# Attention and a top-1 mixture of experts on one core: the last batch's slots enter the slot product as one-hot matmuls, and the table of the other batches is read during attention

## The chip, the cores and the metric

One Trainium2 chip, one of its cores. The metric is the device time in microseconds (us) of one execution; lower is better. The core has TensorE (PE in the profile, with its weight loads as PEld), VectorE (DVE), ScalarE (ACT), GpSimd (POOL) and the sync engine SP, which issues most of the transfers.

## The reference

Four batches of eight heads attend over 768 positions with a cluster mask; the result, 3,072 tokens of 512 numbers, goes through a mixture of 16 experts in 4 groups, one expert per token.

```python
mask = q_assign[:, :, :, None] == k_assign[:, :, None, :]
scores = np.where(mask, scale * q @ k.T, -1e9)
attn = softmax(scores);  x = (attn @ v) as [3072, 512]
g_idx = argmax(x @ w_group);  g_w = softmax(x @ w_group)[g_idx]
e_idx = argmax(x @ w_expert[g_idx]);  e_w = softmax(...)[e_idx]
out = g_w * e_w * (relu(x @ w1[g, e]) @ w2[g, e])
```

## The kernel before

**Attention and routing.** The batches are attended one after the other. After each batch its 768 tokens (6 blocks of 128, one token per partition) are routed in `Router.decide`: the group and expert logits give a one-hot row of 16 experts per token (`roe`, 128 x 6 x 16), a matmul with triangular ones gives each token's rank within its expert (`psm<-roe,low`, and `psm<-roe,ones`), VectorE adds the expert's base (`rps`), and the row number in a table is the sum (`rds`, as integers `rdi`). Six indirect transfers on GpSimd's queue (`table<-pay,rdi`, L685) write token number and gate (`pay`) into that row. The table lies in device memory, one stretch of rows per expert.

**The first expert.** After batch 2 of 0 to 3 is routed, `Experts.first` chooses the expert f0 with the most tokens so far, loads its weights in four chunks for each of w1 and w2 while batch 3 is attended, reads its rows of the table (`tabA`, then integers `idA`), gathers its tokens and transposes them (`xTA`). Once batch 3 is attended, `part_a` runs f0's layers on these tokens (288 columns): 8 groups of 12 matmuls `psh<-xTA` (L963), each closed by a ScalarE eviction `hh` (L965, the upper half of the split number) and a VectorE eviction `hl` (L966, the lower half, which needs `hh`); then 4 groups of 24 matmuls `psy` (L985) over 288 columns. `psh` has three PSUM banks: a fourth group needs a bank that an earlier group's `hl` has read.

**What runs beside it.** Batch 3 is routed at the same time (`decide(B - 1, early=X.order)`); its tokens of f0 become one-hot rows in `slots_b` (`st`, 6 of 128x128 on VectorE, L1107; `o16` on ScalarE) and are collected by matmuls in `tokens_b`. `order` ranks the other 15 experts by their load (`gt`, `rank`, `pr`, `pe`, `ef`, `ei`, `perm`); `ei` is read by SP, whose loads of the later experts' weights (`st<-w`, L767) need it.

**The slot product.** `slots_b` ends with the read of the first 384 rows of every expert from the table (`tb`, L1113). The read waits for all scatters, those of batch 3 too. `slots`, called at step 13 of the 16 (0 to 15) of `part_a`'s loop, multiplies `tb` by the permutation `perm` (`psm<-perm,tb`, L1143: 6 matmuls in f32, 12 in the trace), which gives for every rank and row a token number and a gate as columns (`ri`, `rg`), and these drive the gathers `xg<-xbuf,ri` (L925) of the next expert.

**Order.** The program is written in one sequence, and a scheduler fixes each engine's order when the kernel is built: it moves instructions of `part_a` ahead of `decide` and `slots_b` where their buffers allow it. A tile name is a ring of buffers (`hh` has two), handed out in the order of the code. At run time each engine's instructions start in the built order, except that weight loads may run ahead.

Of the kernel before, what the change touches and what calls it, by code (L numbers as in the profile page):

```python
# [11 lines left out]
F16 = mybir.dt.float16  # L12
BF16 = mybir.dt.bfloat16
F32 = mybir.dt.float32
I32 = mybir.dt.int32
AF = mybir.ActivationFunctionType
ALU = mybir.AluOpType
AX = mybir.AxisListType
# [4 lines left out]
P = 128  # L23
# [6 lines left out]
PSM = "psm"  # L30
FIRST = 2
LAND = 4

def attention(ctx, tc, qT, kT, vr, cen, R, DEN, cfg):
    nc = tc.nc
# [493 lines left out]
class Router:  # L529
# [98 lines left out]
    def decide(self, b, early=None, then=None):  # L628
        nc, sm, E = self.nc, self.sm, self.E
        T = self.N // self.B // P  # L630
        t0 = b * T
# [7 lines left out]
        nc.vector.tensor_reduce(out=mw, in_=eq, axis=AX.X, op=ALU.max)  # L639
        nc.vector.tensor_tensor(out=oh, in0=eq, in1=mw.broadcast_to([P, G, 4]), op=ALU.is_equal)  # L640
        oh = oh.rearrange("p (t g) x -> p t g x", g=5)
        oe = sm.tile([P, T, 4, 4], F16, name="roe")
        og = sm.tile([P, T, 4], F32, name="rog")
        nc.vector.tensor_copy(out=og, in_=oh[:, :, 0])
        nc.vector.tensor_tensor(out=oe, in0=oh[:, :, 1:5], in1=og.broadcast_to([P, T, 4, 4]), op=ALU.mult)
# [34 lines left out]
        for c in range(T):  # L680
# [3 lines left out]
            with self.tc.issue_after(self.cfg["lo"].ins) if self.apart and not early and "lo" in self.cfg else ExitStack():  # L684
                d = self.last["p"] = nc.gpsimd.indirect_dma_start(  # L685
                    out=self.table, out_offset=bass.IndirectOffsetOnAxis(ap=di[:, c:c + 1], axis=0),
                    in_=self.pay[:, t0 + c], in_offset=None)
# [21 lines left out]
class Experts:  # L709
# [95 lines left out]
    def first(self):  # L805

        nc, R, E = self.nc, self.R, self.R.E
        t = self.small("ft", [P, E])
        m = self.small("fm", [P, 1])
        nc.vector.tensor_tensor(out=self.cntA, in0=R.cb, in1=R.ebase, op=ALU.subtract)  # L810
        nc.vector.scalar_tensor_tensor(out=t, in0=self.cntA, scalar=float(2 * E), in1=self.io, op0=ALU.mult, op1=ALU.subtract)
        nc.vector.tensor_reduce(out=m, in_=t, axis=AX.X, op=ALU.max)
        nc.vector.tensor_scalar(out=self.oh0, in0=t, scalar1=m, scalar2=None, op0=ALU.is_equal)
        nc.vector.tensor_tensor(out=t, in0=self.oh0, in1=self.io, op=ALU.mult)
        nc.vector.tensor_reduce(out=self.f0f, in_=t, axis=AX.X, op=ALU.add)
        nc.vector.tensor_copy(out=self.f0i, in_=self.f0f)

        nc.vector.tensor_scalar(out=t, in0=R.cb, scalar1=-1.0, scalar2=float(E * R.BS), op0=ALU.mult, op1=ALU.add)
        nc.vector.tensor_tensor(out=t, in0=t, in1=self.oh0, op=ALU.mult)
        nc.vector.tensor_tensor(out=R.cb, in0=R.cb, in1=t, op=ALU.add)  # L820
        yield
        self.f0 = self.load_reg(self.f0i[0:1, 0:1], E - 1)
        self.WA = self.wtiles(self.wa, 0)
        chunks = []
        for q in range(4 + LAND):
            if q < 4:
                chunks.append(self.load_chunk(0, self.f0, q))
            if q >= LAND:
                yield from self.split_beside(chunks[q - LAND], *self.WA, 0, q - LAND)
            for _ in range(FIRST):  # L830
                yield

        CA, KD = self.CA, R.KD
        nt = -(-CA // P)
        sz = [min(P, CA - t * P) for t in range(nt)]
        tab = self.small("tabA", [P, nt, 2])
        tv = R.table.rearrange("(e s) w -> e s w", s=R.BS)[bass.ds(self.f0, 1)].rearrange("e s w -> (e s) w")
        w2A = [self.load_chunk(1, self.f0, q) for q in range(4)]
        self.WA += self.wtiles(self.wa, 1)
        while R.done < R.B - 2:  # L840
            yield
        for t, n in enumerate(sz):
            R.reads(nc.sync.dma_start(out=tab[0:n, t], in_=tv[t * P:t * P + n]))
        for _ in range(FIRST + 8):
            yield
        ids = self.small("idA", [P, nt], I32)
        g = self.small("gA", [P, nt])
        for t, n in enumerate(sz):
            nc.vector.tensor_copy(out=ids[0:n, t:t + 1], in_=tab[0:n, t, 0:1])
            nc.vector.tensor_scalar(out=g[0:n, t:t + 1], in0=tab[0:n, t, 1:2], scalar1=1.0 / (XS * WS * WS), scalar2=None, op0=ALU.mult)  # L850
        self.colsA = [g[0:n, t:t + 1] for t, n in enumerate(sz)], [ids[0:n, t:t + 1] for t, n in enumerate(sz)]

# [207 lines left out]
    def order(self):  # L1060

        nc, R, E = self.nc, self.R, self.R.E
        sm = self.small
# [6 lines left out]
        nc.vector.scalar_tensor_tensor(out=key, in0=self.oh0, scalar=-1e7, in1=key, op0=ALU.mult, op1=ALU.add)  # L1070
        gt = sm("gt", [P, E, E], F16)
        nc.vector.tensor_tensor(out=gt, in0=key.unsqueeze(1).broadcast_to([P, E, E]), in1=key.broadcast_to([P, E, E]), op=ALU.is_gt)
        rank = sm("rank", [P, E])
        nc.vector.tensor_reduce(out=rank, in_=gt, axis=AX.X, op=ALU.add)
        pr = self.pr = sm("pr", [1, E, E])
        iob = self.io[0:1].broadcast_to([1, E, E])
# [12 lines left out]
        perm = sm("perm", [E, E])  # L1089
# [4 lines left out]
    def slots_b(self):  # L1094
        nc, R, E = self.nc, self.R, self.R.E

        T = R.rows.shape[1]
# [10 lines left out]
        nc.scalar.copy(out=self.o16, in_=o32)  # L1108
        self.o32, self.pb = o32, pb
        next(self.fill)  # L1110
        nt = self.nt = -(-max(self.caps) // P)
        self.tb = self.stage2.tile([P, 2, 512], F32, name="tb", bufs=1).rearrange("p a b -> p (a b)")[0:E, 0:2 * nt * P].rearrange("e (s w) -> e s w", w=2)
        R.reads(nc.sync.dma_start(out=self.tb, in_=R.table.rearrange("(e s) w -> e s w", s=R.BS)[0:E, 0:nt * P]))  # L1113

    def tokens_b(self):

# [19 lines left out]
    def slots(self):  # L1136

        nc, R, E, perm, tb, nt = self.nc, self.R, self.R.E, self.perm, self.tb, self.nt
        tps = self.R.psm.tile([P, 512], F32, name="psm")
        tpv = tps[:, 0:2 * nt * E].rearrange("p (w t e) -> p w t e", w=2, t=nt)  # L1140
        for t_ in range(nt):
            for w in range(2):
                nc.tensor.matmul(out=tpv[:, w, t_], lhsT=tb[:, t_ * P:(t_ + 1) * P, w], rhs=perm, start=True, stop=True)  # L1143
        self.ids, self.gates = self.columns([tpv[:, 0], tpv[:, 1]], [P, nt, E], "r")
        self.xg0 = self.gathers(0)

# [229 lines left out]
def tile_cluster_attention_moe(ctx, tc, qT, kT, vr, cen, wr, w1, w2, out):  # L1376
# [32 lines left out]
    ga = X.part_a()  # L1409
    for _ in R.decide(B - 1, early=X.order):  # L1410
        pass
    X.slots_b()
    for i, _ in enumerate(ga):
        with tc.issue_after(X.mm.ins):
# [42 lines left out]
```

## Time and profile before

| | us |
|---|---|
| median of 3 runs | 775.78 (771.64 to 777.94) |
| span of the profiled execution | 768.7 |
| time of the profiled execution | 770.8 |
| PE busy in it | 724.7 (94%) |
| DVE busy | 598.9 (78%) |
| POOL busy | 495.7 (64%) |
| ACT busy | 444.6 (58%) |
| 416.8 to 443.9: PE busy | 26.76 of 27.10 |
| 443.9 to 449.15: PE busy | 0.00 of 5.25 |

Attention ends at about 416.8 us; `part_a` and the routing of batch 3 fill 416.8 to 457.3 us, and the other fifteen experts the rest. Each row of a timeline gives the start, the time from first start to last end of a run of like instructions, engine, line, operation, what it writes and reads, and in brackets the idle time before it with what ended that. On VectorE and TensorE instructions overlap in the pipeline, so the step from one start to the next is what each costs in a queue without gaps.

### The profile page before, as it was taken

To read this page: it belongs to the slowest core of one execution; us is meant where nothing else is said; L and a number is where in the kernel's file an instruction comes from. 1 tells how busy PE (TensorE), PEld (TensorE's weight loads), DVE (VectorE), ACT (ScalarE), POOL (GpSimd) and SP (SyncE) were. 2 spreads that over 40 slices of the span, in tenths; PEclk is the share of its full clock that TensorE was granted. 3 is DMA by queue.
4 is the path that set the end of the run, shared out by engine and by line. 5 is a ranking of instruction groups with operands and counts; after the bars stand their busy time and mean duration, and the time that the engine had idled before them with its cause. 6 is when DMAs were issued, how large, how long until landed. Compare 5 with 4: busy or idle time off the path is not lost. (4 is left out here: it accounts for less than half of the span.)

```text
span 768.7 us, 26315 instructions
## 1 busy us (share of the span) xinstructions
PE 724.7 (94%) x10882; PEld 619.0 (81%) x10882; DVE 598.9 (78%) x1194; ACT 444.6 (58%) x877; POOL 495.7 (64%) x522
## 2 busy tenths in 40 slices
PE   5898999999999999997898979999999999999996
PEld 3676888888888888876776857888779999999896
DVE  5997988899798988996665545868588988888761
ACT  4567867677686777755674246444534455555542
POOL 9568687889978998787852435426555555554433
PEclk9999999999999999999989979999999999999998
DMA  8759647467653765407422487866677788788721
GB/s 248 190 157 217 161 125 158 111 145 185 125 162 91 173 146 104 97 12 178 127 63 61 55 269 275 275 210 216 226 245 239 255 255 274 256 279 276 248 75 49
DMA packets 115719, 134.75 MB, mean 175 GB/s; under 512 B 34963, under 2 KB 85651, under 8 KB 115592
## 3 DMA queue, kind: packets, MB, share of 16 engines
q1 hardware_dynamic: 109820, 119.61, 56.7%
q0 software_dynamic: 5616, 13.35, 4.9%
q8 instruction: 87, 1.43, 0.8%
q14 instruction: 40, 0.33, 0.2%
q10 hardware_dynamic: 156, 0.03, 0.0%
HBM read 93.20 MB, written 14.11 MB: 140 GB/s over the span
## 5 line engine op out<-in xcount | busy, mean ns | idle before, releaser
L354 POOL TENSOR_TENSOR pl<-p 128x512 f16<-128x512 f32 x278 | 285.6, 1047 | 80.8 <-ACT p L352 75.8
L308 DVE TENSOR_REDUCE mpart<-psc 128x1 f32<-128x512 f32 (+1 forms) x282 | 190.0, 683 | 29.2 <-PE psc L305 28.5
L352 ACT ACTIVATE p<-psf 128x512 f32<-128x512 f32 x288 | 168.5, 593 | 76.5 <-PE psf L348 69.4
L373 PE MATMUL pso<-V,p 128*128 128x65 f16 x1152 | 164.0, 195 | 0.0
L373 PE MATMUL pso<-V,pl 128*128 128x65 f16 x1152 | 163.2, 195 | 0.0
L374 PE MATMUL pso<-V,p 128*128 128x64 f16 x1152 | 162.9, 192 | 0.0
L374 PE MATMUL pso<-V,pl 128*128 128x64 f16 x1152 | 162.6, 192 | 0.0
L347 PE MATMUL psf<-A 82*128 82x384 f16 (+2 forms) x576 | 145.9, 278 | 6.4 <-ACT p L352 3.8
L348 PE MATMUL psf<-B 128*128 128x384 f16 (+2 forms) x576 | 146.1, 278 | 0.0
L374 PEld LDWEIGHTS <-p 128*128 128x128 bf16 x1152 | 113.6, 99 | 21.1 <-issue 1.0
L373 PEld LDWEIGHTS <-p 128*128 128x128 bf16 x1152 | 113.2, 98 | 12.6 <-issue 4.6
L305 PE MATMUL psc<-A 80*128 80x512 f16 (+1 forms) x376 | 109.9, 334 | 5.3 <-DVE mpart L308 4.2
L374 PEld LDWEIGHTS <-pl 128*128 128x128 f16 x1152 | 113.7, 99 | 0.6 <-issue 0.2
L373 PEld LDWEIGHTS <-pl 128*128 128x128 f16 x1152 | 112.1, 97 | 0.3
L966 DVE SCALAR_TENSOR_TENSOR hl<-psh,hh 128x160 f16<-128x160 f32 (+14 forms) x136 | 50.2, 371 | 60.5 <-ACT hh L965 60.1
L965 ACT ACTIVATE hh<-psh 128x160 f16<-128x160 f32 (+14 forms) x136 | 46.5, 347 | 62.5 <-PE psh L963 62.2
L963 PE MATMUL psh<-xT,wh0a 128*128 128x288 f16 (+7 forms) x512 | 74.7, 255 | 0.0
L348 PEld LDWEIGHTS <-B 128*128 128x128 f16 x576 | 57.4, 100 | 15.8 <-issue 6.6
L925 POOL DMA_INDIRECT xg<-xbuf,ri x32 | 42.2, 1318 | 40.9 <-issue 19.8
L963 PE MATMUL psh<-xT,wh0b 128*128 128x272 f16 (+6 forms) x448 | 65.2, 254 | 1.3 <-DVE xT L937 0.7
L347 PEld LDWEIGHTS <-A 82*128 82x128 f16 x576 | 56.2, 99 | 11.5 <-DMA A<-mr 2.2
L963 PE MATMUL psh<-xT,wl0a 128*128 128x288 f16 (+7 forms) x256 | 64.0, 255 | 0.0
(303 smaller groups left out, 1688.4 us busy)
## 6 DMA issues: line engine op xcount, KB each, us to landing
st<-w SPq DMA_DIRECT2D x128, 512.0 KB
B<-parts SPq DMA_DIRECT2D x64, 192.0 KB
kx<-kT SPq DMA_DIRECT2D x16, 384.0 KB
qx<-qT SPq DMA_DIRECT2D x16, 384.0 KB
vx<-vr SPq DMA_DIRECT2D x16, 384.0 KB
A<-parts SPq DMA_DIRECT2D x32, 192.0 KB
xbuf<-xs SPq DMA_DIRECT2D x16, 384.0 KB
A<-mk SPq DMA_DIRECT2D x56, 24.0 KB
```

The lines of the kernel that those rows point to most:

```text
L305: last["mm"] = nc.tensor.matmul(out=pc[:, off:off + k1 - k0], lhsT=QA[h % 8][0:80, c * P:(c + 1) * P], rhs=KA[h % 8][0:80, k0:k1], start=T ...
L308: nc.vector.tensor_reduce(out=(mp[:, 0, 0:1], mp[:, :, 1], mp[:, 1, 0:1])[i], in_=pc.rearrange("p (a x) -> p a x", a=n), axis=AX.X, op=ALU ...
L347: nc.tensor.matmul(out=o, lhsT=KA[h % 8][0:82, ks], rhs=QA[h % 8][0:82, q0:q1], start=True, stop=False)
L348: nc.tensor.matmul(out=o, lhsT=KBs[h][:, ks], rhs=QBs[h][:, q0:q1], start=False, stop=True)
L352: cfg["exp"] = nc.scalar.activation(out=p32, in_=pf, func=AF.Exp, scale=QK / (SQ * SQ))
L354: lo = (nc.vector if u in (EARLY if h < 2 else DVE_LO[h % 8] if h < NH - 2 else DVE_END) else nc.gpsimd).tensor_tensor(out=pl, in0=p32, in ...
L373: nc.tensor.matmul(out=O[:, col:col + 65], lhsT=p[:, bs], rhs=vh, start=c == 0 and q == 0 and i == 0, stop=False, skip_group_check=True)
L374: nc.tensor.matmul(out=O[:, col:col + 64], lhsT=p[:, bs], rhs=vl, start=False, stop=c == NCH - 1 and i == 1, skip_group_check=True)
L925: self.got = nc.gpsimd.indirect_dma_start(out=xg[0:n].rearrange("p k a x -> p (k a x)"), out_offset=None, in_offset=bass.IndirectOffsetOnA ...
L963: self.mm = nc.tensor.matmul(out=ph[:, 0:M], lhsT=w[:, k, fs], rhs=xT[:, a, k], start=i == 0, stop=i == 3 * KD - 1)
L965: nc.scalar.activation(out=hh[:, f], in_=ph[:, 0:M], func=AF.Relu)
L966: self.ev = nc.vector.scalar_tensor_tensor(out=hl[:, f], in0=ph[:, 0:M], scalar=0.0, in1=hh[:, f], op0=ALU.max, op1=ALU.subtract)
```

## The change

- `tb` is no longer read after the last scatters. It is read in `first`, during the attention of batch 3, right behind `tabA`; it waits only for the scatters of the batches before, and holds no row of batch 3. Both reads come `SENT` = 4 steps of the attention loop later than before, and the steps behind them are 4 fewer.
- `slots_new`, called between `decide` and `slots_b`, makes the missing rows from what VectorE holds: `oS`, one row of 288 per token that is 1 at the token's row within its expert (6 comparisons 128x288 with a 128-wide scalar per block, in a buffer of the `hh` ring), and `sw`, one row of 16 ranks per token times token number and gate, each in three parts that bf16 holds (128x576).
- `slots` adds 54 small matmuls (3 row tiles x 6 blocks x 3 parts, 32 columns each) into the same PSUM tile as the six of `perm` and `tb`.
- The loads of f0's w2 chunks are written one after each split of a w1 chunk, no longer all four behind the last.

```diff
+SENT = 4
@@ first
-        chunks = []
+        chunks, w2A = [], []
...
+            if q >= LAND:
+                w2A.append(self.load_chunk(1, self.f0, q - LAND))
...
-        w2A = [self.load_chunk(1, self.f0, q) for q in range(4)]
         self.WA += self.wtiles(self.wa, 1)
         while R.done < R.B - 2:
             yield
+        for _ in range(SENT):
+            yield
         for t, n in enumerate(sz):
             R.reads(nc.sync.dma_start(out=tab[0:n, t], in_=tv[t * P:t * P + n]))
-        for _ in range(FIRST + 8):
+        nt = self.nt = -(-max(self.caps) // P)
+        self.tb = self.small("tb", [R.E, nt * P, 2])
+        R.reads(nc.sync.dma_start(out=self.tb, in_=R.table.rearrange("(e s) w -> e s w", s=R.BS)[0:R.E, 0:nt * P]))
+        for _ in range(FIRST + 4):
             yield
@@ slots_b: the allocation and read of tb are taken out
+    def slots_new(self):
...
+        io = self.small("io16", [P, S], F16)
+        nc.gpsimd.iota(io, [[1, S]], base=0, channel_multiplier=0, allow_small_or_imprecise_dtypes=True)
...
+        x = self.small("sx", [P, T, E])
+        nc.vector.tensor_tensor(out=x, in0=oe, in1=R.ebase.unsqueeze(1).broadcast_to([P, T, E]), op=ALU.mult)
+        s = self.small("sslot", [P, T])
+        nc.vector.tensor_reduce(out=s, in_=x, axis=AX.X, op=ALU.add)
+        nc.vector.tensor_tensor(out=s, in0=R.rows, in1=s, op=ALU.subtract)
+        self.oS = self.xp.tile([P, T, S], F16, name="hh")
+        for c in range(T):
+            nc.vector.tensor_scalar(out=self.oS[:, c], in0=io, scalar1=s[:, c:c + 1], scalar2=None, op0=ALU.is_equal)
...
+        nc.vector.tensor_tensor(out=x, in0=oe, in1=self.rank.unsqueeze(1).broadcast_to([P, T, E]), op=ALU.mult)
+        rho = self.small("srank", [P, T])
+        nc.vector.tensor_reduce(out=rho, in_=x, axis=AX.X, op=ALU.add)
+        nc.vector.tensor_tensor(out=x, in0=self.io.unsqueeze(1).broadcast_to([P, T, E]), in1=rho.broadcast_to([P, T, E]), op=ALU.is_equal)
+        self.sw = self.small("sw", [P, T, 6, E], BF16)
+        nc.vector.tensor_tensor(out=self.sw, in0=x.unsqueeze(2).broadcast_to([P, T, 6, E]), in1=vals.rearrange("p t i w -> p t (i w)").broadcast_to([P, T, 6, E]), op=ALU.mult)
@@ slots
-                nc.tensor.matmul(out=tpv[:, w, t_], lhsT=tb[:, t_ * P:(t_ + 1) * P, w], rhs=perm, start=True, stop=True)
+                nc.tensor.matmul(out=tpv[:, w, t_], lhsT=tb[:, t_ * P:(t_ + 1) * P, w], rhs=perm, start=t_ + w == 0, stop=False, skip_group_check=True)
+        for t_ in range(nt):
+            for c in range(T):
+                for i in range(3):
+                    lhsT = self.oS[:, c, t_ * P:min((t_ + 1) * P, self.oS.shape[2])]
+                    nc.tensor.matmul(out=tpv[0:lhsT.shape[1], :, t_], lhsT=lhsT, rhs=self.sw[:, c, 2 * i:2 * i + 2], start=False, stop=c == T - 1 and i == 2, skip_group_check=True)
@@ main
+    X.slots_new()
     X.slots_b()
```

The built order of the two kernels differs at three places, shown as rows of that order; lines of the changed kernel stand a little lower in the file (L973 there is L966 here, L970 is L963, L1114 is L1107).

VectorE, from the end of the routing of batch 3, in the kernel before (`hl` is the eviction of `part_a`, `yl` that of its second layer; `xN` counts equal rows in a row):

```order
L1107 TENSOR_SCALAR st<-sl,rds 128x128
L1077 TENSOR_TENSOR pr<-rank,io 1x256
L1086 TENSOR_TENSOR dg<-rank,identf 16x16
L966 SCALAR_TENSOR_TENSOR hl<-psh,hh 128x288
L1079 TENSOR_TENSOR pe<-pr,io 1x256
L1088 TENSOR_REDUCE rc<-dg 16x1
L966 SCALAR_TENSOR_TENSOR hl<-psh,hh 128x288
L1081 TENSOR_REDUCE ef<-pe 1x16
L1090 TENSOR_SCALAR perm<-io,rc 16x16
L1083 CAST ei<-ef 1x16
L966 SCALAR_TENSOR_TENSOR hl<-psh,hh 128x288 x2
L989 SCALAR_TENSOR_TENSOR yl<-psy,yh 128x288 x2
```

The same place in the changed kernel:

```order
L1090 CAST ei<-ef 1x16
L1139 TENSOR_SCALAR hh<-io_11141,sslot 128x288
L1142 TENSOR_TENSOR sg<-pay,svals 128x6
L1146 TENSOR_TENSOR sx<-roe,rank 128x96
...
L1148 TENSOR_REDUCE srank<-sx 128x6
...
L1149 TENSOR_TENSOR sx<-io,srank 128x96
L1114 TENSOR_SCALAR st<-sl,rds 128x128
L1151 TENSOR_TENSOR sw<-sx,svals 128x576
L1114 TENSOR_SCALAR st<-sl,rds 128x128 x4
L973 SCALAR_TENSOR_TENSOR hl<-psh,hh 128x288 x8
L996 SCALAR_TENSOR_TENSOR yl<-psy,yh 128x288 x2
```

Before, four of the eight `hl` stand ahead of `rps` and the other four between the rows of `order`; now all eight stand in one run behind the last row of the routing, of `slots_new` and of `slots_b`.

TensorE, around the rank matmuls of batch 3, before (with what each row waits for):

```order
L963 MATMUL psh<-xTA,wl_9285 128x288
L662 LDWEIGHTS low
L662 MATMUL psm<-roe,low 128x96 [waits DVE_49]
L664 LDWEIGHTS ones
L664 MATMUL psm<-roe,ones 128x80
...
L666 MATMUL psm<-roe,ones 128x16
L963 LDWEIGHTS wh_9284
L963 MATMUL psh<-xTA,wh_9284 128x288
```

And in the changed kernel:

```order
L970 MATMUL psh<-xTA,wl_9285 128x288
L663 LDWEIGHTS low
L663 MATMUL psm<-roe,low 128x96 [waits DVE_49]
...
L667 MATMUL psm<-roe,ones 128x16
L992 LDWEIGHTS wh_10114 [waits DMASW3_49,DMASW2_49,DMASW4_49,DVE_49,PE_49]
L992 MATMUL psy<-hh,wh_10114 128x288 [waits Activation_49]
...
L970 LDWEIGHTS wh_9284
L970 MATMUL psh<-xTA,wh_9284 128x288 [waits DVE_49]
```

Before, 54 `psh` matmuls (four and a half groups) stand ahead of the rank matmuls and more follow at once; now 36 (three groups) stand ahead, six `psy` follow, and the 37th `psh` waits for VectorE.

SP, from the end of the table reads of attention on, in the changed kernel:

```order
L847 DMA tabA<-table 128x2
L335 DMA A_171<-mr 1x6x128
L847 ISA
L847 DMA tabA<-table 32x2
L850 DMA tb<-table 16x768
L335 DMA A_172<-mr 1x6x128
L875 DMA_TRANSPOSE xTA<-qx 128x8x128
...
L804 TENSOR_LOAD ei
L804 ISA x2
L768 ISA
L768 DMA st<-w 128x2x512
```

Before, `tb<-table` stood behind the fifth `st<-w` of the stream; now it stands here, behind one row `A<-mr` and the third `tabA`. The rows of f0's w2 loads ahead of this place (L767 before, L768 now, 128x4x256) stand in the same order in both kernels. Fourteen of the loads of `ei`, which stood between later weight loads, now stand between the fifth and the sixth.

## Rows read from the trace of the kernel before

**Rows 1.** The waits of TensorE from 416 to 470 us: who waited, on what, us in total, how often, longest.

```profile
PE psm L1143 <- DMA tb<-table: 5.3, 1, 5.3
```

**Rows 2.** The chain of waits that ended last, from 434 to 458 us: start, us, what.

```profile
434.80 11.10 DMA table<-pay,rdi
...
446.01 3.01 DMA tb<-table
...
449.15 2.71 PE psm L1143 x12
451.86 5.45 PE psy L985 x24
```

**Rows 3.** Busy time of each engine in stretches around that wait: the stretch and its length, then busy us and instructions of PE, PEld, DVE, ACT and POOL, the granted TensorE clock as a share of 2.4 GHz, the share of the DMA engines and GB/s.

```profile
416.80:443.90 27.10, 26.76 (x273) 21.24 (x269) 14.38 (x57) 9.19 (x18) 8.40 (x10) 1.00 0.42 80
443.90:449.15 5.25, 0.00 (x0) 0.03 (x1) 1.88 (x4) 2.79 (x4) 0.00 (x0) 0.74 0.87 226
...
452.00:455.00 3.00, 3.00 (x14) 1.93 (x13) 2.85 (x5) 0.00 (x0) 1.71 (x2) 0.50 0.56 164
455.00:458.00 3.00, 3.00 (x28) 2.26 (x27) 0.23 (x1) 0.67 (x2) 2.39 (x3) 0.72 0.86 299
```

**Rows 4.** TensorE's timeline just ahead of that wait.

```profile
440.94 1.45 PE L1129 MATMUL psm<-pb,st 128*128 128x2 f32 x12
442.25 0.65 PE L985 MATMUL psy<-hh,wl 128*128 128x288 f16 x4
442.74 1.14 PE L985 MATMUL psy<-hl,wh 128*128 128x288 f16 x8
```

**Rows 5.** TensorE's timeline around the rank matmuls of batch 3, 425 to 430 us.

```profile
425.07 0.20 PE L662 MATMUL psm<-roe,low 128*128 128x96 f16 x1
...
425.41 0.41 PE L963 MATMUL psh<-xTA,wh 128*128 128x288 f16 x2
...
429.08 1.02 PE L985 MATMUL psy<-hh,wh 128*128 128x288 f16 x7
```

**Rows 6.** VectorE's timeline from 423 to 432 us, rows of the routing of batch 3 and of part_a.

```profile
423.86 0.46 DVE L966 SCALAR_TENSOR_TENSOR hl<-psh,hh 128x288 f16<-128x288 f32 x1 [0.19 <-ACT hh L965]
...
424.76 0.26 DVE L645 TENSOR_TENSOR roe<-psm,rog 128x96 f16<-128x96 f32 x1
...
425.59 0.26 DVE L669 TENSOR_TENSOR rps<-psm,cb 128x96 f32<-128x96 f32 x1
...
428.07 0.42 DVE L1072 TENSOR_TENSOR gt<-key 128x256 f16<-128x256 f32 x1
428.41 0.18 DVE L1103 COPY pb<-pay 128x6 f32<-128x6 f32 x1
428.50 0.27 DVE L1107 TENSOR_SCALAR st<-sl,rds 128x128 f32<-128x128 f32 x1
...
429.03 0.42 DVE L1107 TENSOR_SCALAR st<-sl,rds 128x128 f32<-128x128 f32 x1
429.22 0.41 DVE L1077 TENSOR_TENSOR pr<-rank,io 1x256 f32<-1x256 f32 x1
...
429.64 0.44 DVE L966 SCALAR_TENSOR_TENSOR hl<-psh,hh 128x288 f16<-128x288 f32 x1
430.01 0.40 DVE L1079 TENSOR_TENSOR pe<-pr,io 1x256 f32<-1x256 f32 x1
...
431.24 0.16 DVE L1083 CAST ei<-ef 1x16 int32<-1x16 f32 x1
```

**Rows 7.** VectorE's timeline at 417 us, one row whose input and output are f16 and the row behind it.

```profile
417.20 0.20 DVE L883 TENSOR_SCALAR back<-ident 128x128 f16<-128x128 f16 x1
417.31 0.17 DVE L1102 TENSOR_SCALAR pb<-pay 128x6 f32<-128x6 f32 x1
```

**Rows 8.** The same view of stretches as rows 3, for three us soon after another wait of TensorE, and that wait and the restart in TensorE's timeline.

```profile
409.00:412.00 3.00, 3.00 (x26) 2.13 (x25) 1.18 (x2) 2.04 (x5) 1.85 (x2) 0.50 0.00 0
...
407.50 0.41 PE L963 MATMUL psh<-xTA,wh 128*128 128x288 f16 x2 [2.38 <-DMA xTA<-vx]
```

**Rows 9.** TensorE's timeline in attention, a run of the router's small matmuls and the row behind it.

```profile
412.97 0.60 PE L609 MATMUL psm<-WR,xTr 128*128 128x20 f16 x18
413.43 0.22 PE L347 MATMUL psf<-A 82*128 82x128 f16 x1
```

**Rows 10.** The first use of the slot product on VectorE, the first and the third gather that follow on GpSimd, and the matmuls that transpose the gathered rows on TensorE (timelines of the three engines).

```profile
451.90 0.21 DVE L1053 CAST ri<-psm 128x48 int32<-128x48 f32 x1 [6.12 <-PE psm L1143]
...
452.99 1.60 POOL L925 DMA_INDIRECT xg<-xbuf,ri  x1 [15.09 <-issue]
...
456.15 0.88 POOL L925 DMA_INDIRECT xg<-xbuf,ri  x1 [0.30 <-issue]
...
462.21 1.35 PE L935 MATMUL psm<-ident,xg 128*128 128x128 f16 x24
```

**Rows 11.** Busy time in later stretches, columns as in rows 3.

```profile
470.00:600.00 130.00, 129.94 (x1162) 106.73 (x1160) 98.61 (x145) 57.33 (x109) 64.35 (x54) 1.00 0.73 235
...
615.00:690.00 75.00, 74.94 (x924) 74.34 (x922) 64.53 (x100) 39.84 (x85) 43.96 (x41) 1.00 0.84 265
690.00:735.00 45.00, 43.09 (x597) 42.28 (x594) 37.59 (x59) 22.95 (x54) 21.42 (x22) 1.00 0.81 266
```

**Rows 12.** VectorE's timeline during the attention of batch 3, at the first use of tabA.

```profile
382.77 0.15 DVE L849 CAST idA<-tabA 128x1 int32<-128x1 f32 x1 [4.10 <-DMA tabA<-table]
```

More of the change, by code (lines that the diff above doesn't have):

```diff
@@ L641, in decide @@
         oh = oh.rearrange("p (t g) x -> p t g x", g=5)
-        oe = sm.tile([P, T, 4, 4], F16, name="roe")
+        oe = self.oe = sm.tile([P, T, 4, 4], F16, name="roe")
         og = sm.tile([P, T, 4], F32, name="rog")
@@ L1072, in order @@
         nc.vector.tensor_tensor(out=gt, in0=key.unsqueeze(1).broadcast_to([P, E, E]), in1=key.broadcast_to([P, E, E]), op=ALU.is_gt)
-        rank = sm("rank", [P, E])
+        rank = self.rank = sm("rank", [P, E])
         nc.vector.tensor_reduce(out=rank, in_=gt, axis=AX.X, op=ALU.add)
@@ L1110, in slots_b @@
         next(self.fill)
-        nt = self.nt = -(-max(self.caps) // P)
-        self.tb = self.stage2.tile([P, 2, 512], F32, name="tb", bufs=1).rearrange("p a b -> p (a b)")[0:E, 0:2 * nt * P].rearrange("e (s w) -> e s w", w=2)
-        R.reads(nc.sync.dma_start(out=self.tb, in_=R.table.rearrange("(e s) w -> e s w", s=R.BS)[0:E, 0:nt * P]))
+    def slots_new(self):
+        nc, R, E = self.nc, self.R, self.R.E
+        T = R.rows.shape[1]
+        t0 = R.N // P - T
+        S = max(self.caps)
+        oe = R.oe.rearrange("p t g x -> p t (g x)")
+        io = self.small("io16", [P, S], F16)
+        nc.gpsimd.iota(io, [[1, S]], base=0, channel_multiplier=0, allow_small_or_imprecise_dtypes=True)
+        vals = self.small("svals", [P, T, 3, 2], BF16)
+        nc.gpsimd.memset(vals, 0.0)
+        nc.gpsimd.iota(vals[:, :, 0, 0], [[P, T]], base=-P * T, channel_multiplier=0, allow_small_or_imprecise_dtypes=True)
+        nc.gpsimd.iota(vals[:, :, 1, 0], [[0, T]], base=0, channel_multiplier=1, allow_small_or_imprecise_dtypes=True)
+        x = self.small("sx", [P, T, E])
[6 more added lines that the diff above has]
+            nc.vector.tensor_scalar(out=self.oS[:, c], in0=io, scalar1=s[:, c:c + 1], scalar2=None, op0=ALU.is_equal)
+        g = self.small("sg", [P, T])
+        nc.vector.tensor_copy(out=vals[:, :, 0, 1], in_=R.pay[:, t0:t0 + T, 1])
+        nc.vector.tensor_tensor(out=g, in0=R.pay[:, t0:t0 + T, 1], in1=vals[:, :, 0, 1], op=ALU.subtract)
+        nc.vector.tensor_copy(out=vals[:, :, 1, 1], in_=g)
+        nc.vector.tensor_tensor(out=g, in0=g, in1=vals[:, :, 1, 1], op=ALU.subtract)
+        nc.vector.tensor_copy(out=vals[:, :, 2, 1], in_=g)
+        nc.vector.tensor_tensor(out=x, in0=oe, in1=self.rank.unsqueeze(1).broadcast_to([P, T, E]), op=ALU.mult)
[4 more added lines that the diff above has]
+        nc.vector.tensor_tensor(out=self.sw, in0=x.unsqueeze(2).broadcast_to([P, T, 6, E]), in1=vals.rearrange("p t i w -> p t (i w)").broadcast_to([P, T, 6, E]), op=ALU.mult)
@@ L1142, in slots @@
             for w in range(2):
-                nc.tensor.matmul(out=tpv[:, w, t_], lhsT=tb[:, t_ * P:(t_ + 1) * P, w], rhs=perm, start=True, stop=True)
+                nc.tensor.matmul(out=tpv[:, w, t_], lhsT=tb[:, t_ * P:(t_ + 1) * P, w], rhs=perm, start=t_ + w == 0, stop=False, skip_group_check=True)
+        T = R.rows.shape[1]
+        for t_ in range(nt):
[3 more added lines that the diff above has]
+                    nc.tensor.matmul(out=tpv[0:lhsT.shape[1], :, t_], lhsT=lhsT, rhs=self.sw[:, c, 2 * i:2 * i + 2], start=False, stop=c == T - 1 and i == 2, skip_group_check=True)
         self.ids, self.gates = self.columns([tpv[:, 0], tpv[:, 1]], [P, nt, E], "r")
```

## The prediction

> **What bounds the kernel now.** I read the waits of TensorE first, then the chain that ended last, then the windows, then the timelines of the engines that meet there. Of all that TensorE waits for between 416 and 470 us one wait counts, 5.3 us of the slot product for `tb` [rows 1]. The chain says what is behind it: the last scatter takes 11.10 us to land, the read of `tb` starts at 446.01 only then, and the twelve f32 matmuls and 24 `psy` that follow take 2.71 and 5.45 us [rows 2]. Ahead of the wait TensorE is busy for 26.76 of 27.10 us at full clock, in it not at all; after it the granted clock is 0.50 (1.2 GHz) from 452 to 455 us and 0.72 to 458 [rows 3]. At full clock such work is cheaper: twelve f32 matmuls take 442.25 - 440.94 = 1.31 us, four `psy` 442.74 - 442.25 = 0.49, which is 0.1225 us each [rows 4]. So the wait costs 5.27 us by the end of `psy` before and the start behind (5.3 in the view), and the low clock (2.71 - 1.31) + (5.45 - 24 x 0.1225) = 1.4 + 2.5 = 3.9 us. From 470 to 600 and from 615 to 690 us TensorE is busy to within 0.1 us each, from 690 to 735 to within 1.9 [rows 11]: what is won or lost at 417 to 460 us arrives at the end almost whole, and at most some 2 us of a loss can be swallowed there.
>
> **What the change removes.** `tb` now waits for scatters of earlier batches alone and is read next to `tabA`, whose first use is at 382.77 [rows 12], 66 us ahead of the slot product at 449.15 [rows 2]. The 5.27 us go, and with them the cause of that low clock: -5.3 and -3.9.
>
> **What it moves.** The built order shows a price on the other side. `oS` takes a buffer of the `hh` ring ahead of `part_a`, and all eight `hl` now stand behind the routing, `slots_new` and `slots_b` on VectorE. Before, four stood ahead of `rps` and four in between. TensorE has three `psh` banks; its 37th `psh` needs the first `hl`. I work out when that comes.
>
> When VectorE gets there. `roe` started at 424.76, behind an `hl` at 423.86 that had 0.19 us of idle ahead of it and steps by 430.01 - 429.64 = 0.37 [rows 6]. Without these 0.56 us it starts at 424.20, and `rps`, 0.83 us behind it before, at 425.03. From `rps` (425.59) to the start of `ei` (431.24) are 5.65 us [rows 6]; two `hl` of 0.37 stand in it, and `ei` itself adds 0.08 (the estimate for a tiny row; `pb` of 128x6 steps by 0.09), so the old chain without `hl` is 5.0 us. It contains the six `st`.
>
> What `slots_new` adds to it. Six rows of 128x6 at 0.09 us are 0.5. Four of 128x96, between 0.09 and the 0.34 of `gt` 128x256 (428.41 - 428.07), I take at 0.2: 0.8. `sw`, 128x576, goes by the slope between `st` 128x128 (429.22 - 429.03 = 0.19) and `gt`: 0.34 + 320/128 x 0.15 = 0.7 [rows 6]. The six one-hots of 128x288 are dear or cheap: by that slope 0.19 + 160/128 x 0.15 = 0.38 each as f32 rows, and not below the 0.11 of the f16 `back` 128x128 (417.31 - 417.20) [rows 7]. They read and write f16, so I take 0.2, nearer to that row: 1.2 us, with ends 0.7 and 2.3. Sum 5.0 + 0.5 + 0.8 + 0.7 + 1.2 = 8.2 us, from 7.7 to 9.3. The first `hl` starts at 425.03 + 8.2 = 433.2 and takes 0.44 [rows 6]: the 37th `psh` runs at about 433.7, between 433.2 and 434.8.
>
> A rule weighed. The one-hots at 0.11 to 0.38 are the only durations here with a page against them. The Trainium skill, "VectorE: DVE Perf Modes", says in its mode table that a `tensor_scalar` in 16 bits within SBUF handles four elements a cycle, and in its errata section that such an instruction takes 58 cycles and the elements over that factor, at 0.96 GHz: an estimate of 0.135 us each, 0.8 in all instead of 1.2, and the sum below would be +6.0 instead of +6.4. The same page gives f32 rows a factor of two, an estimate of 0.13 us for `st`, where the trace has 0.19 [rows 6]; so the trace does not bear it out throughout.
>
> What TensorE does until then. Before, the row behind the rank matmuls came at 425.41, with 54 `psh` done [rows 5]. Now 36 are done, so 18 x 0.1225 = 2.2 us of that work is not there, and six `psy` (0.74 us; seven go in 1.02 with the last one's drain [rows 5]) are. Without any wait the work ahead of the 37th `psh` would end at 425.41 - 2.2 + 0.74 = 423.95. TensorE therefore idles 433.7 - 423.95 = 9.8 us, from 9.2 to 10.9, of which about 1.6 us lie ahead of the rank matmuls (425.07 - 2.2 = 422.87, and `roe` has to be there) and the rest behind them. ScalarE's `hh` of the first three groups wait no longer than that. The `psh` and `psy` that were to hide the routing are the same matmuls as before; they only come later.
>
> The clock after it. The restart follows an idle time longer than the 5.27 us that cost 3.9. The lower bound is a wait of 2.38 us at 407.50, after which the clock was 0.50 for all of 409 to 412: 1.5 us lost at the least [rows 8]. The nearest row is the long wait, so I take 3.9.
>
> What it adds on TensorE. 54 matmuls of 32 columns. Eighteen of 20 columns took 413.43 - 412.97 = 0.46 us, 26 ns each [rows 9]: 1.4 us, and twice that, 2.8, as the upper end. Nothing hides them.
>
> The gathers. They start once `ri` is there: `ri` at 451.90, third gather issued at 456.15, its rows used at 462.21 without an idle time ahead [rows 10]. Those 10.3 us held the 24 `psy` at half clock; at full clock they hold 2.5 us less. How much of that was slack the trace does not say: 0 to 2.5, and I take 0.5 because the transposes did not wait.
>
> What costs nothing. The scatters still run on GpSimd, and nobody waits for `table` at that point now. The fourteen `ei` loads stand between the fifth and the sixth weight load, where SP stood waiting for the scatters until 446.01 [rows 2]; the cover is that wait, and the sixth load is no later than before as long as they take under some 10 us. The w2 loads of f0 stand in the same order on SP: 0. The read of `tb` in attention stands behind reads for which VectorE waits 4.10 us anyway [rows 12].
>
> **Sum.** -5.3 - 3.9 + 9.8 + 3.9 + 1.4 + 0.5 = +6.4 us. With all lower ends: -9.2 + 9.2 + 1.5 + 1.4 = +2.9; with all upper ends: -9.2 + 10.9 + 3.9 + 2.8 + 2.5 = +10.9. The profiled execution took 770.8 us, so it becomes 777.2. It lies 5.0 us under the median of the runs (775.78), so the median becomes 782.2, I say 782.
>
> **Rivals.**
> Faster: the first `hl` is no bound, and only the removed wait is left, with the 54 matmuls: -5.3 - 3.9 + 1.4 = -7.8, 768.0 for the median. For it speaks that the wait for `tb` is certain to go. Against it, the order on VectorE is fixed and TensorE has only three banks. The point that decides is when the first `hl` ends: with equal clocks the account is even at 5.3 - 1.4 - 0.5 = 3.4 us of new idle time, so at 427.3 us; `rps` at 425.03 leaves 2.3 us for a chain of which 5.0 are old rows.
> Slower still: the one-hots go at the f32 price and the third gather is late, which TensorE then waits for a second time: 6.4 + 1.1 + 2.0 = +9.5, 785.3. For it speaks that the transposes had no idle time before; it decides when VectorE's chain exceeds 9 us and the gathered rows land later than 24 full-clock `psy` allow.
> No difference: the later reads in attention are there when VectorE asks. The 4.10 us of VectorE [rows 12] shrink and with them the wait of 2.38 us and at least 1.5 us of low clock [rows 8], at most -4.10 - 2.38 - 1.5 = -8.0 against +6.4: -1.6, 774.2. Against it: the conversion of `tabA` stands as close behind the read as before.
>
> **How the numbers follow.** Forecast 0.58, with 778.7 to 786.7 as its own range; slower still 0.17; faster 0.13; no difference 0.12. One per cent, 7.8 us, is about what a measurement of this kernel can tell from no change. The forecast's +6.4 lies inside it, and about 0.17 of its 0.58 above. So: faster 0.13 and a little of the rest, 0.15; slower 0.17 + 0.17 = 0.34; same 0.51. The range reaches from 770, which takes in "no difference" and leaves out most of "faster", to 788, above the upper ends by about one.
>
> **What the changed profile would show.** TensorE's waits from 416 to 470 us: none on `tb`; instead `psh` waiting for `hl`, 7.5 to 9.5 us in one piece that ends at 433 to 435 us. VectorE's timeline: eight `hl` in a row behind `st`, no idle time of note from `rps` to them, one-hots stepping by about 0.2. Windows: clock 0.50 for several us after the restart, and not after 447. The 54 matmuls in about 1.4 us. Wrong I would be if the first `hl` came before 428 us, or if the clock stayed at 1.00 after the idle time, which alone would be worth 3.9 us.

## The result and the profile after

The changed kernel takes 779.68 us (median of 20 runs, 774.37 to 783.15), the kernel before 772.62 us on the same chip (20 runs, 766.40 to 779.58): a ratio of 1.008 over the runs, 95% interval 1.0059 to 1.0101, so about 6.2 us slower (the two medians differ by 7.1). The prediction said +6.4 us. In every ratio here, runs more than 1.5% above the fastest of the same kernel are left out as disturbed. The profiled execution of the changed kernel has a span of 776.4 us against 768.7, a time of 778.2 against 770.8.

The waits of TensorE from 405 to 475 us in the changed kernel, the largest four (who waited, on what, us in total, times, longest); they answer to [rows 1]:

```profile
PE psh L970 <- DVE hl L973: 8.3, 4, 6.8
PE psh L970 <- DMA xTA<-vx: 2.4, 1, 2.4
PE psm L663 <- DVE roe L646: 1.0, 1, 1.0
PE psy L992 <- ACT hh L972: 0.9, 1, 0.9
```

The wait on `tb` is gone. In its place stands one of 6.8 us on the first `hl`, with 1.0 us ahead of the rank matmuls and 0.9 us ahead of the six `psy`; the wait for `xTA` is the old one [rows 8].

VectorE's timeline of the changed kernel, the rows that answer to [rows 6]:

```profile
424.22 0.26 DVE L646 TENSOR_TENSOR roe<-psm,rog 128x96 f16<-128x96 f32 x1
...
425.12 0.26 DVE L670 TENSOR_TENSOR rps<-psm,cb 128x96 f32<-128x96 f32 x1 [0.16 <-PE psm L667]
...
427.47 0.30 DVE L1139 TENSOR_SCALAR hh<-io,sslot 128x288 f16<-128x288 f16 x1
427.68 0.42 DVE L1079 TENSOR_TENSOR gt<-key 128x256 f16<-128x256 f32 x1
...
432.22 0.76 DVE L1151 TENSOR_TENSOR sw<-sx,svals 128x576 bf16<-128x576 f32 x1
432.90 0.94 DVE L1114 TENSOR_SCALAR st<-sl,rds 128x128 f32<-128x128 f32 x4
433.68 1.18 DVE L973 SCALAR_TENSOR_TENSOR hl<-psh,hh 128x288 f16<-128x288 f32 x3
```

`roe` starts at 424.22, `rps` at 425.12, and from there VectorE works without a gap until the first `hl` at 433.68, 8.56 us later. A one-hot steps by 0.21 us here (427.68 - 427.47), `sw` by 0.68.

TensorE's timeline of the changed kernel at the same place and at the slot product; it answers to [rows 4] and [rows 5]:

```profile
425.92 1.42 PE L992 MATMUL psy<-hh,wh 128*128 128x288 f16 x6 [0.91 <-ACT hh L972]
...
434.19 0.64 PE L970 MATMUL psh<-xTA,wh 128*128 128x288 f16 x2 [6.84 <-DVE hl L973]
...
456.60 1.58 PE L1181 MATMUL psm<-perm,tb 16*128 16x16 f32 x12
...
458.12 1.61 PE L1187 MATMUL psm<-sw,hh 128*128 128x32 bf16 x54
...
459.66 1.54 PE L992 MATMUL psy<-hh,wh 128*128 128x288 f16 x8
```

The 37th `psh` runs at 434.19, half a microsecond behind the start of the first `hl`. The slot product no longer waits, and the 54 new matmuls take 459.66 - 458.12 = 1.54 us, 28.5 ns each.

The windows of the changed kernel (columns as in [rows 3]), at the new wait and behind the slot product:

```profile
430.00:434.00 4.00, 0.00 (x0) 0.00 (x0) 4.00 (x21) 0.13 (x1) 3.21 (x3) 0.50 0.30 9
...
436.00:438.00 2.00, 2.00 (x11) 1.23 (x9) 0.29 (x1) 0.41 (x1) 1.21 (x1) 0.50 1.20 91
438.00:440.00 2.00, 2.00 (x11) 1.31 (x10) 0.16 (x1) 0.00 (x0) 0.00 (x0) 0.55 0.29 90
440.00:442.00 2.00, 2.00 (x19) 1.61 (x17) 0.49 (x2) 0.82 (x2) 0.00 (x0) 1.00 1.05 374
...
458.00:460.00 2.00, 2.00 (x59) 1.86 (x59) 1.47 (x3) 1.01 (x2) 0.00 (x0) 1.00 0.80 277
460.00:462.00 2.00, 2.00 (x12) 1.27 (x11) 1.22 (x2) 0.00 (x0) 1.24 (x1) 0.57 0.63 219
462.00:464.00 2.00, 2.00 (x11) 1.30 (x10) 0.00 (x0) 0.00 (x0) 1.39 (x3) 0.58 0.78 215
```

From 430 to 434 us VectorE is the busy engine (4.00 of 4.00) and TensorE does nothing. The granted clock, as a share of 2.4 GHz, is 0.50 (1.2 GHz) until about 439.8 us. It is 1.00 again from 440 us, and falls a second time at about 460 us, behind the slot product, although TensorE has been busy for 2.00 of 2.00 us there.

What both cost stands in the chain of waits of the changed kernel (start, us, what):

```profile
434.19 10.24 PE psh L970 x60
...
459.72 4.73 PE psy L992 x24
```

At 0.1225 us each [rows 4] the 60 `psh` would take 7.35 us and the 24 `psy` 2.94: about 2.9 us lost behind the wait and 1.8 behind the slot product. (From start to start, without the drain of the last matmul in each run, it is 2.7 and 1.7.)

### The profile page after: what moved, and what is told of

Its sections match the earlier page's. It is cut to its first block, busy times and chain, and to the rows that moved or that the text cites. A ratio compares the mean times of both kernels' runs of the same rounds, so it can differ in the third digit from the quotient of the medians.

```text
span 776.4 us, 26446 instructions
## 1 busy us (share of the span) xinstructions
PE 728.6 (94%) x10936; PEld 621.4 (80%) x10936; DVE 602.4 (78%) x1212; ACT 445.2 (57%) x877; POOL 496.4 (64%) x526
## 4 chain that ended last, share of the span: by engine, by line
PE 66%; DVE 10%; DMA 7%; ACT 6%; issue 5%; POOL 4%; SPq 1%; POOLq 0%; ACTq 0%; DVEq 0%
PE psh L970 16%; PE psy L992 13%; PE pso L374 6%; PE psf L348 6%; PE psf L349 6%; PE pso L375 5%; PE psc L306 5%; PE psy L1006 3%; DVE mpart L309 2%; DMA B<-parts 2%; ACT p L353 2%; DMA st<-w 2%; PE psm L1032 1%; POOL pl L355 1%; PE psm L942 1%
## 5 line engine op out<-in xcount | busy, mean ns | idle before, releaser
L973 DVE SCALAR_TENSOR_TENSOR hl<-psh,hh 128x160 f16<-128x160 f32 (+14 forms) x136 | 50.2, 371 | 70.5 <-ACT hh L972 58.6
L970 PE MATMUL psh<-xT,wh0a 128*128 128x288 f16 (+7 forms) x512 | 74.7, 255 | 0.0
L970 PE MATMUL psh<-xT,wh0b 128*128 128x272 f16 (+6 forms) x448 | 65.2, 254 | 1.3 <-issue 0.8
L970 PE MATMUL psh<-xT,wl0a 128*128 128x288 f16 (+7 forms) x256 | 64.0, 255 | 0.0
```

The source lines that it names most:

```text
L970: self.mm = nc.tensor.matmul(out=ph[:, 0:M], lhsT=w[:, k, fs], rhs=xT[:, a, k], start=i == 0, stop=i == 3 * KD - 1)
L973: self.ev = nc.vector.scalar_tensor_tensor(out=hl[:, f], in0=ph[:, 0:M], scalar=0.0, in1=hh[:, f], op0=ALU.max, op1=ALU.subtract)
```

## The experiments

The theory: the loss comes from `hl`. `oS` takes the first buffer of the `hh` ring, so `part_a`'s `hh` and with it all `hl` are ordered behind the routing and the new chain on VectorE. Rivals: the new work itself and later gathers; the reads moved in attention; the low clock as the main cost. Each ratio is to the kernel before on the same chip.

**The ring, the place of the call, and the bare removal.** Three kernels. The first gives `oS` a buffer of another ring:

```diff
-        self.oS = self.xp.tile([P, T, S], F16, name="hh")
+        self.oS = self.xp.tile([P, T, S], F16, name="xT")
```

> The changed kernel with one edit: the one-hot rows oS take a buffer of the xT ring in place of the hh ring; all its work stays. Theory (the loss comes from hl standing behind VectorE's new chain because of the shared ring): 54 psh instead of 36 stand ahead of the rank matmuls again, four hl ahead of rps, the other four still behind the chain. TensorE then has 30 psh and 14 psy of work after the rank matmuls and waits about 4 us for the fifth hl instead of 6.8 for the first; the waits for roe and for hh go. Against the kernel before: about 0 us, from -3 to +2; against the changed kernel about -7. Rival 1 (the loss comes from the new work itself: the 54 matmuls, the longer VectorE queue and the later gathers): the ring changes little, still +5 to +8 against before. Rival 2 (the loss comes from the reads moved in attention): +5 to +8 as well, with waits ahead of 417 us that the kernel before lacks.

The second has this edit too, and calls `slots_new` in the loop:

```diff
-    X.slots_new()
     X.slots_b()
     for i, _ in enumerate(ga):
+        if i == 7:
+            X.slots_new()
```

> As the run before, and the one-hot chain is also called later, at step 7 of the loop of part_a, so that it stands behind the last routing rows and behind seven of the eight hl on VectorE; all work of the change stays. Theory: no wait of TensorE over 1 us between 417 and 450 us, none on tb, the chain hides behind psy. Against before: -5.3 of wait, -3.9 of low clock, +1.5 for the 54 matmuls, +0 to +4 for a later fall of the clock and for later gathers: -4 to -8 us, 0.990 to 0.995. Rival 1 (new work and late gathers): 0 to +4 us. Rival 2 (reads in attention): 0 to +6 us.

The third leaves out the call and the 54 matmuls, and so the last batch's rows:

```diff
-    X.slots_new()
...
-        T = R.rows.shape[1]
-        for t_ in range(nt):
-            for c in range(T):
-                for i in range(3):
...
```

> The changed kernel without slots_new and without the 54 matmuls: what is left out are the last batch's rows in the slot product, so its tokens of the later experts are gathered as empty rows. What stays: tb read in attention, the w2 loads. It measures what the removal of the wait is worth by itself. Theory: hl stand between the routing rows as in the kernel before, no wait on tb, clock 1.00 through 417 to 457 us: -5.3 - 3.9 = -9.2 us, or up to 2.5 us less if the gathers now make TensorE wait: -6.7 to -9.2 us against before, 0.988 to 0.991. Rival 1 (wait replaced by the next one, on the gathers): -2 to -5 us. Rival 2 (reads in attention cost): 0 to -3 us.

Measured: the ring alone 766.84 against 768.25 us, 0.9979 (0.9950 to 1.0009); ring and late call 761.03, 0.9925 (0.9893 to 0.9957); no one-hots 763.27, 0.9952 (0.9922 to 0.9983).

TensorE's timeline of the first: 14 `psy` behind the rank matmuls' `psh`, then the wait that was expected (3.4 us, about 4 expected) for the fifth `hl` and not for the first:

```profile
429.62 1.88 PE L992 MATMUL psy<-hh,wh 128*128 128x288 f16 x14
434.87 0.41 PE L970 MATMUL psh<-xTA,wh 128*128 128x288 f16 x2 [3.38 <-DVE hl L973]
```

In the second the one-hots follow seven `hl`, and this is what VectorE's timeline shows of the last four of them, with the row behind:

```profile
434.45 0.90 DVE L1139 TENSOR_SCALAR xT<-io,sslot 128x288 f16<-128x288 f16 x4
435.27 0.18 DVE L1143 CAST svals<-sg 128x6 bf16<-128x6 f32 x1
```

Four take 435.27 - 434.45 = 0.82 us, 0.205 each. The two largest groups of TensorE's waits from 416 to 480 us in this version:

```profile
PE psh L970 <- DVE hl L973: 0.8, 2, 0.5
PE psm L1181 <- DVE xT L1164: 0.6, 1, 0.6
```

All the work of the change is in it, so neither the new work nor the reads in attention make it slow, and those two rivals fall. The theory holds: an edit of one name takes the loss away (the interval of the first version includes 1), and the place of the call makes a gain of it.

The bare removal won less than was expected: 3.7 us (1.3 to 6.0) where 6.7 to 9.2 were on record. The size is that of the rival with a new wait, 2 to 5 us, though the wait is more on the weights than on the gathers. Its waits of TensorE from 416 to 480 us:

```profile
PE psm L1032 <- ACT xT L944: 1.5, 1, 1.5
PE psm L1181 <- DVE xT L1164: 0.9, 1, 0.9
PE psm L942 <- DMA xg<-xbuf,ri: 0.7, 1, 0.7
```

and the chain behind the first two of them:

```profile
432.29 8.46 DMA st<-w
440.78 1.06 ACT wh0a L775
441.87 1.23 DVE wl0a L778
443.09 0.61 DVE xT L1164
...
448.35 9.64 DMA st<-w
458.01 1.06 ACT wh0b L775
459.07 0.48 ACT xT L944
```

A load of the first weights starts at 432.29, as early as `ei` lets it. Its split on ScalarE and VectorE stands ahead of the copy `xT` for which the slot product waits; the same happens once more 16 us later, from a load that took 9.64 us. In the kernel before, the slot product stood until 449.15 us for `tb`, and this did not show. And the clock fell behind the slot product here too: 24 `psy` from 445.26 to 449.88, 4.6 us instead of 2.9. It fell once more behind the second of these waits, to 0.50 from 460 to 462 us, so the two falls and the waits on weights are what the -9.2 us, the best end of the expectation, had left out.

**The clock, and where the slot product stands.** Four kernels, the first of them the changed kernel again.

> The changed kernel itself, unedited, on the chip on which the next three run: +5 to +8 us against the kernel before, as in its first measurement (ratio 1.008); the measure for the run with filled idle time.

The second fills TensorE's wait with matmuls whose result nothing reads:

```diff
+        if early:
+            fill = self.psm.tile([P, 512], F32, name="psm")
+            xr = self.cfg["xs"][:, 0, 0:2].rearrange("p c a x -> p (c a x)")
+            for i in range(34):
+                nc.tensor.matmul(out=fill, lhsT=self.ones, rhs=xr, start=True, stop=True)
         ps = sm.tile([P, T, E], F32, name="rps")
```

> The changed kernel, and behind the rank matmuls of batch 3 34 matmuls 128x512 into a PSUM tile that nothing reads, about 7.3 us of work that fills TensorE's wait for the first hl; the wait for hl itself, and all later work, stay. Theory (the low clock behind the wait is a cost of its own, caused by the idle time): the granted clock stays 1.00 from 434 to 440 us, 60 psh take 7.4 us instead of 10.2, so about -2.9 us against the changed kernel, ratio to before 1.002 to 1.006; the fall behind the slot product (460 us) stays, 1.8 us, since it has no idle time ahead. Rival (the clock falls there for another reason, or what it gives back is taken by the next wait): the same time as the changed kernel, within 1 us.

The third and the fourth are the version with ring and late call, with other steps:

```diff
     SLOTS = 13
-    SLT = 12
+    SLT = 10
```

> The version with oS in the xT ring and the one-hot chain late, and the last batch's own tokens are collected at step 10 instead of 12 of the loop, so that 36 psy instead of 12 lie between those small matmuls and the slot product; same work. In that version the granted clock fell to 0.50 about 2 us behind the slot product without a wait of note. If runs of small matmuls close to each other bring the clock down (theory): the clock stays 1.00 to 455 us, the 24 psy behind the slot product take 2.9 instead of 4.7 us, and the wait of the slot product for the xT copy (0.6 us) goes: -1 to -2.5 us against that version, ratio to before 0.988 to 0.992. Rival (the slot product alone does it, or the start of the weight loads bounds this stretch): the same as that version, 0.992 to 0.994.

```diff
-    SLOTS = 13
-    SLT = 12
+    SLOTS = 10
+    SLT = 13
```

> The version with oS in the xT ring and the one-hot chain late, and the slot product is taken at step 10 and the last batch's tokens at step 13 of the loop; same work. The gathers then start some 6 to 8 us earlier against the matmuls that use them. If late gathers or the xT copy behind a weight split cost time in that version: -1 to -3 us against it, ratio 0.987 to 0.992, with no wait of the slot product on VectorE. Rival (bound by weight loads, splits and evictions from 450 us on): the same, 0.991 to 0.994; or slower, if the last batch's tokens now come late for the first psh behind part_a: up to +3 us.

Measured: the changed kernel 773.15 against 767.76 us, 1.0079 (1.0051 to 1.0108); filled 771.57, 1.0062 (1.0030 to 1.0094); tokens apart 762.96, 0.9881 (0.9815 to 0.9947); slots early 763.27, 0.9956 (0.9925 to 0.9986). The third has six runs, and its ratio rests on three of them (751.13, 760.16 and 762.02 us), so it says little; the median of all six is 0.994 of the kernel before, like that of the fourth, and its profiled execution took 764.59 us.

With the filling the clock stays at 1.00. The window of it, and the same one of the changed kernel beside it (second fence):

```profile
434.00:437.00 3.00, 2.58 (x22) 2.06 (x22) 1.55 (x5) 1.24 (x2) 2.68 (x5) 1.00 1.00 71
```

```profile
434.00:437.00 3.00, 3.00 (x20) 2.08 (x19) 0.46 (x1) 0.60 (x2) 0.84 (x1) 0.73 0.79 130
```

From the rank matmuls to the 37th `psh` the two take the same 9.64 us (434.42 - 424.78 and 431.82 - 422.18), and from there to the slot product 19.68 us filled and 21.54 not (454.10 - 434.42, 453.36 - 431.82): 1.9 us is what the low clock behind this wait costs in this execution of the changed kernel, where it lasted to about 435.6 us; in the first profile it was 2.7 by the same account (456.60 - 434.19 = 22.41). The medians differ by 1.6 us, and the intervals overlap, so the time alone does not decide between the theory and its rival; the traces show the low clock gone. With TensorE kept busy the clock does not fall, so it is the idle time that brings it down here. But the filled version is still 4.8 us slower than the kernel before by its ratio: the wait, not the clock, carries the greater part of the loss.

Tokens apart: the clock held to 466 us and the slot product did not wait, as expected; by the median the gain did not show in the time, and what bounded it then reads as in the kernel without one-hots. The chain of it:

```profile
448.50 1.14 DVE wl0a L778
449.65 0.02 issue
449.66 9.16 DMA st<-w
458.82 0.02 issue
458.85 1.06 ACT wh0b L775
459.90 0.48 ACT xT L944
```

Slots early removed the slot product's wait on the copy as well, and its chain has the same load (448.69, 9.44 us) ending in the same copy. With the tokens apart TensorE still waited 1.4 us for gathered rows, with the slots early not at all, and it was no faster. So the chains name the first weights as the bound of these versions, not the gathers and not the clock, and the times do not speak against the rival on record for both.

**The call alone, and the first weights earlier.** Three kernels. The first is the changed kernel with only the call moved into the loop at step 7, and `oS` left in the `hh` ring.

> The changed kernel with one edit: slots_new is called at step 7 of the loop of part_a and not ahead of slots_b; oS stays in the hh ring, which part_a's hh now enters first. Theory (it is the order in which the ring is handed out that puts all hl behind VectorE's chain): 54 psh stand ahead of the rank matmuls again, no wait of TensorE over 1 us from 417 to 450 us, -4 to -8 us against before (0.990 to 0.995), as with the ring changed and the call late. Rival (sharing the ring costs by itself, since the next hh must wait for the 54 matmuls): a new wait of psh or psy on hh behind the slot product, -3 to +3 us.

The second is the version with ring and late call, with

```diff
+                if r == 0:
+                    er[0] = 0
                 if r not in er and r < self.R.E - 1:
```

> The version with oS in the xT ring and the one-hot chain late, and the weights of the first of the fifteen other experts are loaded with a fixed expert number, so that these loads do not wait for ei and four of them are issued at about 420 us instead of 434; what is left out is the choice of that expert, so its tokens meet the weights of another expert. Theory (what is won at 449 us is partly given back because the first weights bound the stretch from 440 to 465 us): the waits there (the slot product on the xT copy behind a weight split, psm and psh on weights and copies, about 2 to 3 us) go, and the clock may hold; -2 to -4 us against that version, ratio to before 0.985 to 0.990. Rival (the gathers or the splits on ScalarE and VectorE bound it): the same as that version, 0.990 to 0.995.

> The version with oS in the xT ring and the one-hot chain late, again, on the chip of the two runs above, as their measure: 0.990 to 0.995 of the kernel before, as the first time.

Measured: the call alone 763.33 against 766.76 us, 0.9951 (0.9924 to 0.9977); first weights early 760.24, 0.9900 (0.9861 to 0.9938); ring and late call again 762.79, 0.9930 (0.9902 to 0.9957).

The call alone is enough: the `hh` ring is shared as in the change, and no wait of TensorE between 416 and 475 us is longer than 0.9 us. The three largest groups:

```profile
PE psm L942 <- DMA xg<-xbuf,ri: 1.0, 2, 0.6
PE psm L1181 <- DVE xT L1164: 0.9, 1, 0.9
PE psh L970 <- DVE hl L973: 0.8, 2, 0.5
```

So it is the order in which the ring is handed out that costs, and not the sharing. The gain, 3.8 us, lies just under the 4 to 8 that were expected. With the first weights early, SP issues two loads at 417.92 and goes on at 420.75 instead of 433.11, and the waits of TensorE that are left from 416 to 475 us are these:

```profile
PE psh L972 <- DVE hl L975: 0.8, 2, 0.5
PE psm L602 <- ACT xs L394: 0.4, 1, 0.4
PE psm L1034 <- ACT xT L946: 0.3, 1, 0.3
```

The slot product's wait for the copy, 1.4 us in the measure beside it, is gone. In time the step is 2.5 us by the medians, inside what was expected, but the intervals overlap; that the loads bound the stretch is shown by waits and chain, not by the time alone. Behind it the chain runs through ScalarE's splits one after the other (`wh0b` at 451.69 and 452.80, then `wh1b`), so the next bound is close.

Of the versions that do all the work, the ring with the late call was measured twice, at 0.9925 and 0.9930 of the kernel before: it is faster than both kernels, though by under 1% of the kernel before.

The second part of the change was not run apart. With the four w2 loads written back where they were, the built order of all five engines is the same row for row as that of the changed kernel.

## Why the prediction was right, step by step

- **The order on VectorE decides.** Right. The first `hl` started at 433.68 (433.2 said) and the 37th `psh` at 434.19 (433.7, range to 434.8), behind a chain of 8.56 us (8.2 said). The one-hots cost 0.20 to 0.32 us each between other rows and 0.205 in a run (0.2 taken), `sw` 0.68 (0.7). The rule that was weighed, four elements a cycle behind 58 fixed cycles in the Trainium skill, "VectorE: DVE Perf Modes" (mode table and errata section), gave an estimate of 0.135 us. The trace does not agree, with 0.205, and no run tells whether the rate or the fixed part is off. The value taken between the rows of the trace was the better guide.
- **New idle time.** 9.8 us said, 9.2 to 10.9; measured 0.32 + 1.01 + 0.91 + 6.84 = 9.1, the first of them ahead of the router's last matmuls. One piece of 7.5 to 9.5 us was said; it was 6.84, because the wait of the six `psy` for `hh` stands apart from it. The restart came 0.5 us later than said; but the six `psy`, priced at 0.74 us, took 1.42 (425.92 to 427.34) as the clock was already falling, 0.53 from 426 to 428 us, and so filled part of it.
- **The clock behind it.** 3.9 us said, from the wait for `tb`; 2.9 in one profile and 2.0 in the other (10.24 and 9.37 us for the 60 `psh`). The upper end of the range was taken, and that was too much.
- **A second fall of the clock.** Not in the sum. The prediction said that the low clock of 447 to 457 us goes with the wait for `tb`, and that the clock would be 1.00 there; 24 `psy` behind the slot product ran at about half clock all the same, 1.8 us lost. That is a step that failed. With the term above it makes 4.7 us against 3.9: two errors that partly cancel, and that is luck.
- **The new matmuls.** 1.4 said, 1.54 measured.
- **The gathers.** 0.5 said. The transposes did not wait, but the stretch around them did: `psm` on a weight split for 0.9 us and `psh` on `hl` for 1.5 in three waits, 2.4 us where the kernel before had 0.8. That is 1.6, and it is no wait for gathered rows.
- **What was put at nothing.** The sixth weight load (`st<-w`) was said to be no later than before; it was issued at 453.55 us instead of 446.65. SP stood 10.3 us for a weight split on VectorE (`wl0a`) ahead of it, not for the loads of `ei`, which were done at about 443.0. It fell back about as far as the slot product (456.60 instead of 449.15), and no weight load stands in the chain of the changed kernel there, so the price of 0 is not contradicted, but the reason given for it was wrong.
- **The sum.** With what was measured: -5.3 - 3.9 + 9.1 + 4.7 + 1.5 + 1.6 = +7.7 us; the profiled span grew by 7.7, and by the ratio of the runs the loss is 6.2. The terms were off by -0.7, -1.0, +1.8, +0.1 and +1.1 us; the mechanism was right, but that the sum came within 0.2 us of the ratio is luck.
- **"What is won at 417 to 460 us arrives at the end almost whole."** This step failed for gains. The bare removal was priced at -7.8 us in the rival "faster", with the new matmuls; the versions in which that wait is gone and the 54 matmuls are done, ring and late call (twice) and the call alone, win 3.8 to 5.8 us by their ratios. What is missing is missing ahead of 480 us already: from the router's last but one group of logits (`psm<-WR,xTr` x9) to the second run of transposes of gathered rows ring and late call needs 55.05 and 55.72 us (476.94 - 421.89, 476.80 - 421.08), the kernel before 59.76 (480.49 - 420.73), so 4.7 and 4.0 us are won there. In its place stand the waits on weight splits and the second fall of the clock: the first weights cannot be there earlier than `ei` and the loads allow.
- **The rivals.** "Faster" asked for a first `hl` by 427.3; the changed kernel does not have it. "No difference" asked for the waits on `tabA` and `xTA` to shrink; VectorE's for `tabA` grew from 4.10 to 5.42 us, TensorE's for `xTA` is 2.4 us as before. "Slower still" asked for a chain over 9 us; it was 8.56.
- **The order of the w2 loads.** 0 said, on the built order; no run contradicts it and none was made for it.

## What to carry to other kernels

A buffer taken from a ring earlier in the code moves everything that takes the next buffer, on engines that the new code does not touch; look in the built order for what the ring's other users now stand behind, and price the first of them for which a starved engine waits. A wait that is removed is worth what the next one behind it leaves: before pricing it, ask what else comes ready only a few microseconds earlier, here the first weights. If a chain is not needed until later, call it later; here one moved call turned a loss of about 6 us into a gain of about 4.

## What the runs showed of the hardware that was not expected

The granted clock fell to 1.2 GHz behind the slot product in some profiles without an idle time of note ahead of it: in the changed kernel no wait stood within 20 us before it, and TensorE was busy for 2.00 of 2.00 us with runs of small matmuls (48 of 128 columns, 12 in f32, then 12 `psy`, 12 in f32 and 54 of 32 columns). It fell in both profiles of the changed kernel, in that with the ring alone, both of ring and late call, that without one-hots and the filled one; it held with the tokens apart, with the slots early, with the first weights early, and with the call alone. The call alone has the same matmuls in the same sequence as ring and late call. Two rows show the difference, each the first of the 24 `psy`, with the call alone and with ring and late call (second fence):

```profile
448.79 1.15 PE L992 MATMUL psy<-hh,wh 128*128 128x288 f16 x8
```

```profile
448.95 2.10 PE L992 MATMUL psy<-hh,wh 128*128 128x288 f16 x8
```

The wait ahead of the slot product was 0.88 us in the one and 1.37 in the other, but 0.59 in the first profile of ring and late call, where the clock fell as well. So the order of the matmuls does not settle it, and the cause stays open. From start to start the 24 `psy` take 4.4 to 4.6 us in the seven profiles and 2.9 to 3.0 in the other four, so it is worth 1.5 to 1.7 us in this place. It did not show in the time: on the same chip the call alone, where the clock held, took 763.33 us, and ring and late call, where it fell, 762.79.
